# Top-k attention and MLP on one core: when MLP chunks arrive, a scan in place of a merge, and reciprocals on GpSimd

## The chip, the core and the metric

The kernel runs on one core of one Trainium2 chip. The time is the device time of one execution in microseconds (us), the median of several runs. The core has five engines with a queue each: TensorE (PE in the profile; PEld is its loading of weights), VectorE (DVE), ScalarE (ACT), GpSimd (POOL) and SyncE (SP), which here only issues DMA transfers. Each engine works through its own instructions in order; they wait for each other through semaphores.

## What is computed

Attention in which each query keeps only its 32 largest scores, followed by a two-layer MLP. All data is float32.

```python
# q, k, v: (8 batches, 8 heads, 576 positions, 64)
scores = scale * np.matmul(q, k.transpose(0, 1, 3, 2))
kth = np.partition(scores, -32, axis=-1)[..., -32:-31]
scores = np.where(scores >= kth, scores, -1e9)
attn = np.exp(scores - np.max(scores, axis=-1, keepdims=True))
attn = attn / (np.sum(attn, axis=-1, keepdims=True) + 1e-09)
x = (attn @ v) brought to (4608 tokens, 512)
h = x @ w_in                                   # (4608, 2048)
g = np.where(h >= 1, h, np.where(h <= -1, 0.0, (h + 1) ** 2 / 4))
return g @ w_out                               # (4608, 512)
```

## The kernel before

**Tiles and steps.** The 576 positions of a batch are four tiles of 128 and a tail of 64. A step (`steps`, line 471) is 128 queries of two heads. A full tile has four steps (one for each pair of heads); the tails of two batches share one MLP tile, and each tail has two steps, because its 64 queries of two pairs of heads fill 128 partitions. That makes 144 steps. `rounds` (line 462) is the order of the tiles over the pairs of batches.

**One step.** `scores` (line 257): TensorE computes 128x576 scores for each of the two heads, and ScalarE copies them out, scaled, into `s`. `first_top` (line 282) forms `more`, the larger of each pair of scores (score c and score c + 288), finds its 8 largest by VectorE's MAX8, and lets ScalarE take the exponential into `e`. `weights` (line 297) then goes on to the 32 largest of `more`: three rounds of MATCH_REPLACE8, which removes the eight found, and MAX8, which finds the next eight, each for two heads on 128x288. Since only the larger of each pair has been looked at, the smaller ones follow: line 317 forms them, line 320 takes their 8 largest (`seconds`), and lines 321 to 324 merge the two sorted lists. The 32nd largest of the union is the largest of these nine numbers: the 32nd of the first list, and min(first list from its 31st downward in rank, seconds upward) for eight pairs; a 9-element MAX8 for each head finds it (`kth`). The mask (line 330) multiplies `e` by "score at least kth" and sums into `z`.

**The sum's reciprocal.** Lines 335 and 336 add 1e-9 to `z` and take the reciprocal `rz` on VectorE, both on 128x2. After that a step goes one of two ways. While the weights of the MLP are still being converted, and in the last two steps, `by_tensor` is set: ScalarE makes a diagonal matrix of `rz`, and TensorE scales and transposes `e` in one matmul (`transpose_w`). In the other 130 steps GpSimd scales `e` by `rz` (line 343), and `move_w` (line 369) has ScalarE split it in 16-bit halves, writes them to DRAM and reads them back through the transposing DMA into `wT`. `values` (line 381) is the product with v, two steps later, and its result is copied to `xT`, the MLP's input.

**The MLP in chunks.** A chunk (`chunks`, line 462) is one or two tiles of 128 tokens. When its last step has passed `values`, its work is put into `pending`: for each of 16 pieces of the hidden layer, `hidden` (4 blocks of `w_in`, ScalarE and GpSimd for the activation) and, four pieces later, `final` (with `w_out`). A tile is worth 128 units, so there are 36 x 128 = 4608 units in all. A float32 matmul shows as two matmul instructions in the trace.

**The order on the engines** is written out by hand. The loop over steps (line 612) divides each step in 7 slots, and `advance` (line 516) puts in pieces of pending MLP work at the end of each slot. How much is set by `share`:

```python
share = (total - spent) / (n + 2 - m)          # line 619
```

that is, what is left of the MLP, spread over the steps that are left. If `pending` runs out, nothing is put in until the next chunk is complete. `K_TIME` (line 513) is the planner's estimate of the time of a step; it bounds what `advance` puts in, and does not itself wait for anything. In the first steps the weights `w_in` and `w_out`, which arrive as 64-bit numbers, are converted by ScalarE, VectorE and GpSimd along with the attention. At the end a flag says whether the second smallest list was ever too short (`excess`, line 345); a second, plain run follows only then.

Of the kernel before, what the change touches and what calls it, by code (L numbers as in the profile page):

```python
# [10 lines left out]
F32 = mybir.dt.float32  # L11
# [3 lines left out]
AF = mybir.ActivationFunctionType  # L15
ALU = mybir.AluOpType
PSUM = bass.MemoryType.PSUM

TOP_K = 32
LOWEST = -3.0e38  # L20
LARGEST = 3.4028234e38
# [3 lines left out]
def kernel(  # L25
# [10 lines left out]
    nc = tc.nc  # L36
    B, H, S, D = q.shape
    NTOK, DM = out.shape
    DFF = moe_w_in.shape[1]
    P = 128  # L40
# [4 lines left out]
    NT = S // P  # L45
# [6 lines left out]
    NK = DM // P  # L52
    NF = DFF // P
# [5 lines left out]
    const = ctx.enter_context(tc.tile_pool(name="const", bufs=1))  # L59
# [4 lines left out]
    minus = const.tile([P, 1], F32, name="minus")  # L64
# [13 lines left out]
    for i in range(2):  # L78
        v_tails.append([const.tile([P, H, D], F32, name=f"v_tail{i}{x}") for x in range(2)])
        for x in v_tails[i]:  # L80
            nc.gpsimd.memset(x, 0.0)

# [3 lines left out]
    excess = const.tile([P, 2 * n_steps + n_pieces], F32, name="excess")  # L88
# [68 lines left out]
    def run(ctx, paired):  # L157
        xtp = ctx.enter_context(tc.tile_pool(name="xtp", bufs=3))
        stage = ctx.enter_context(tc.tile_pool(name="stage", bufs=2))
        att = ctx.enter_context(tc.tile_pool(name="att", bufs=2))  # L160
# [96 lines left out]
        def scores(st):  # L257
            t, hp, kT, qT = st["t"], st["hp"], st["keys"]["kT"], st["qT"]
            st["s"] = s = att.tile([P, 2, S], F32, name="s", bufs=3)
            for hf in range(2):  # L260
# [9 lines left out]
                                             start=True, stop=True)  # L270
                nc.scalar.activation(s[:, :, c0:c1], sp[:, :, 0:SH], AF.Copy, scale=SCALE)  # L271

        def pairs(st):
            s = st["s"]
            st["more"] = more = att.tile([P, 2, SH], F32, name="more")
            nc.vector.tensor_tensor(out=more, in0=s[:, :, 0:SH], in1=s[:, :, SH:S], op=ALU.max)  # L279


        def first_top(st):
            s = st["s"]
            if paired:
                pairs(st)
            st["tops"] = tops = att.tile([P, 2, TOP_K + 8], F32, name="tops", bufs=3)
            st["e"] = e = att.tile([P, 2, S], F32, name="e", bufs=3)
            nmax = att.tile([P, 2], F32, name="nmax")
            for i in range(2):
                nc.vector.max(out=tops[:, i, 0:8], in_=(st["more"] if paired else s)[:, i, :])  # L290
            nc.scalar.activation(nmax, tops[:, :, 0], AF.Copy, scale=-1.0)
            for i in range(2):
                nc.scalar.activation(e[:, i, :], s[:, i, :], AF.Exp, bias=nmax[:, i:i + 1])  # L293
                yield


        def weights(st, after):
            s, m, tops, e = st["s"], st["m"], st["tops"], st["e"]
            kth = att.tile([P, 2, 8], F32, name="kth", bufs=3)
            if paired:  # L300
                src = rest = less = st["more"]
            else:
                src, rest = s, att.tile([P, 2, S], F32, name="rest", bufs=1)
            for r in range(8, TOP_K, 8):
                for i in range(2):
                    nc.vector.match_replace(out=rest[:, i, :], in_to_replace=tops[:, i, r - 8:r],  # L306
                                            in_values=src[:, i, :], imm_value=LOWEST)
                src = rest
                if r == 8:
                    yield  # L310
                if r + 8 == TOP_K:
                    yield
                    yield from first_top(after) if after is not None else (None, None)
                for i in range(2):
                    nc.vector.max(out=tops[:, i, r:r + 8], in_=src[:, i, :])  # L315
            if paired:
                nc.vector.tensor_tensor(out=less, in0=s[:, :, 0:SH], in1=s[:, :, SH:S], op=ALU.min)  # L317
                seconds = att.tile([P, 2, 8], F32, name="seconds")
                for i in range(2):
                    nc.vector.max(out=seconds[:, i, :], in_=less[:, i, :])  # L320
                nc.vector.tensor_tensor(out=tops[:, :, TOP_K:TOP_K + 8], in0=tops[:, :, TOP_K - 2:TOP_K - 10:-1],
                                        in1=seconds, op=ALU.min)
                for i in range(2):
                    nc.vector.max(out=kth[:, i, :], in_=tops[:, i, TOP_K - 1:TOP_K + 8])  # L324
                last = kth[:, :, 0]
            else:
                last = tops[:, :, TOP_K - 1]
            z = att.tile([P, 2], F32, name="z")
            for i in range(2):
                nc.vector.scalar_tensor_tensor(out=e[:, i, :], in0=s[:, i, :], scalar=last[:, i:i + 1],  # L330
                                               in1=e[:, i, :], op0=ALU.is_ge, op1=ALU.mult,
                                               accum_out=z[:, i:i + 1])
            yield
            rz = att.tile([P, 2], F32, name="rz")
            nc.vector.tensor_scalar(z, z, 1e-9, None, ALU.add)  # L335
            nc.vector.reciprocal(rz, z)  # L336
            if st["by_tensor"]:
                st["rz"] = diag = (late or words).tile([P, 2, P], F32, name="diag", bufs=1)
                for i in range(2):
                    nc.scalar.activation(diag[:, i, :], ident, AF.Copy, scale=rz[:, i:i + 1])  # L340
            else:
                for i in range(2):
                    nc.gpsimd.tensor_scalar(e[:, i, :], e[:, i, :], rz[:, i:i + 1], 1.0, ALU.mult, ALU.mult)  # L343
            if paired:
                nc.gpsimd.tensor_tensor(out=excess[:, 2 * m:2 * m + 2], in0=seconds[:, :, 7], in1=kth[:, :, 0],
                                        op=ALU.subtract)
            yield

# [113 lines left out]
        rounds, chunks = [], []  # L462
        for b in range(0, B, 2):
            a, c, tl = [(b, t) for t in range(NT)], [(b + 1, t) for t in range(NT)], (b, NT)
            if b + 2 < B:
                rounds += a + [tl] + c + [(b + 1, NT)]
                chunks += [a[0:2], a[2:4], c[0:2], c[2:4], [tl]] if b else [[x] for x in a + c + [tl]]
            else:
                rounds += a + [tl, (b + 1, NT)] + c
                chunks += [a[0:2], a[2:4], [tl]] + [[x] for x in c]  # L470
        steps = []
        for b, t in rounds:
            tile_of = (b, t) if t < NT else (b - b % 2, t)
# [4 lines left out]
        n = len(steps)  # L478

        ready = {max(m for m in range(n) if steps[m][3] == ch): ch for ch in range(len(chunks))}  # L480
# [4 lines left out]
        pending = deque()  # L485
        total, spent = sum(len(tiles) for tiles in chunks) * (NK * NF + NF * DM // P), 0
# [23 lines left out]
                inspected += 1  # L510


        K_TIME, PIECE_TIME, UNIT_TIME, SLOTS, EARLY_STEPS, EARLY_SHARE = 10.2, 0.55, 0.218, 7, 4, 32
        pe_time, dve_time, done, scored, ready_at, usable = 9.0, 12.0, {}, {}, {}, {0: 0.0}

        def advance(amount, until):
# [77 lines left out]
        for _ in first_top(state[0]):  # L594
            pass
        next(first)
        begin_at(1)
        next_keys, valued = 1, 0
# [13 lines left out]
        for m in range(n + 2):  # L612
# [3 lines left out]
            elif not early and late is None:  # L616
                conversion.close()
                late = ctx.enter_context(tc.tile_pool(name="late", bufs=1))
            share = (total - spent) / (n + 2 - m)
            top_k, parts = None, [0] * SLOTS  # L620
            if m < n:
                top_k = weights(state[m], state[m + 1] if m + 1 < n else None)
                parts = [1] * SLOTS if early else [1, 1, 0, 1, 1, 1, 1]
                start = max(dve_time, scored[m])
                now_converting = range(SLOTS) if m < EARLY_STEPS else range(0, SLOTS, 2)
                dve_time = start + K_TIME + PIECE_TIME * min(len(now_converting), n_pieces - converted)
                done[m] = dve_time
                state[m]["by_tensor"] = early or m >= n - 2
# [60 lines left out]
    with ExitStack() as inner:  # L689
        run(inner, True)  # L690
    again = nc.values_load(flag[0:1, 0:1], min_val=0, max_val=1)
    with tc.If(again > 0):
        with ExitStack() as inner:
            run(inner, False)
# [27 lines left out]
```

## Time and profile before

| | |
|---|---|
| time, median of 3 runs | 1683.67 us (1682.41 to 1685.46) |
| span of the profiled execution | 1683.5 us |
| TensorE busy | 1549.2 us, 92% |
| VectorE busy | 1550.5 us, 92% |
| ScalarE busy | 1188.2 us, 71% |
| GpSimd busy | 974.8 us, 58% |
| the last mask of a step (VectorE) ends | 1607 us |

Busy time is the time in which an engine had at least one instruction under way, not counting register, branch, semaphore and DMA-issuing instructions. The ends of matmuls are modelled, so a busy TensorE isn't TensorE at its peak. In the page's 40 slices of the span each digit is the busy share in tenths, and PEclk is the clock granted to TensorE in the same way. A row of groups gives line, engine, operation, output and inputs, shape and count, then the busy time of the group in us and the mean of one instruction in ns, then the engine's idle time just before it and what ended most of it. A line of waits names who waited for whom, the total in us, how often, and the longest.

### The profile page before, as it was taken

How to read it: one execution, taken by the hardware profiler on the slowest of the kernel's cores; microseconds unless marked ns; L12 is line 12 of the kernel's file. 1: busy time of each engine (PE TensorE's matmuls, PEld its weight loads, DVE VectorE, ACT ScalarE, POOL GpSimd, SP SyncE). 2: the span in 40 equal slices, each digit the busy share in tenths (PEclk: the TensorE clock that was granted, in tenths of full speed). 3: DMA queues.
4: the chain of work that ended last, by engine and by line, in shares of the span. 5: the costliest groups of instructions: out<-in, count | busy, mean ns of one | idle time of the engine just before them, and what ended most of it. 6: DMA issues, size and time to landing. Idle time of an engine off the chain costs nothing.

```text
span 1683.5 us, 30910 instructions
## 1 busy us (share of the span) xinstructions
PE 1549.2 (92%) x9645; PEld 1050.8 (62%) x9645; DVE 1550.5 (92%) x4875; ACT 1188.2 (71%) x2552; POOL 974.8 (58%) x1720
## 2 busy tenths in 40 slices
PE   5586999999998899979999999979999999999998
PEld 4464666666665666646566766646566666666675
DVE  6999999999999999999999999999999999999922
ACT  5677677777777767777677877767667877767743
POOL 4675677666665554536465755526465765657750
PEclk6698999999998999979999999979999999999999
DMA  9333345455555546554555555554555544544400
GB/s 246 114 98 91 86 132 160 129 151 141 140 154 156 144 135 174 142 157 135 146 159 143 150 142 151 158 158 124 155 150 151 143 131 130 132 133 117 114 27 16
DMA packets 439055, 227.83 MB, mean 135 GB/s; under 512 B 393056, under 2 KB 401248, under 8 KB 438880
## 3 DMA queue, kind: packets, MB, share of 16 engines
q1 hardware_dynamic: 438880, 225.75, 49.4%
q8 instruction: 78, 1.28, 0.3%
q14 instruction: 97, 0.79, 0.2%
HBM read 62.91 MB, written 86.11 MB: 89 GB/s over the span
## 4 chain that ended last, share of the span: by engine, by line
DVE 51%; PE 33%; ACT 7%; issue 3%; POOL 3%; DMA 2%; SPq 1%; DVEq 0%; POOLq 0%; ACTq 0%
PE ph L419 13%; DVE more L306 12%; PE py L444 12%; DVE tops L315 10%; DVE e L330 8%; DVE more L317 4%; DVE seconds L320 4%; DVE tops L290 4%; DVE more L279 4%; PE po L389 3%; PE sp L269 3%; ACT halves L372 2%; ACT e L293 1%; DVE z L335 1%; DVE kth L324 1%
## 5 line engine op out<-in xcount | busy, mean ns | idle before, releaser
L419 PEld LDWEIGHTS ph<-xT,w_in 128*128 128x128 f32 x3328 | 505.1, 195 | 199.0 <-issue 88.5
L419 PE MATMUL ph<-xT,w_in 128*128 128x128 f32 (+1 forms) x3328 | 594.1, 326 | 32.8 <-ACT g L431 18.6
L444 PE MATMUL py<-w_out,g 128*128 128x512 f32 x1152 | 564.3, 605 | 2.0 <-POOL w_out L136 1.8
L423 ACT ACTIVATE r<-ph,half 128x128 f32<-128x128 f32 (+1 forms) x416 | 169.7, 408 | 292.9 <-PE ph L419 237.6
L306 DVE MATCH_REPLACE8 more<-tops,more 128x288 f32<-128x288 f32 x864 | 375.6, 442 | 0.0
L436 POOL TENSOR_SCALAR r<-r 128x128 f32<-128x128 f32 (+1 forms) x392 | 164.9, 421 | 343.4 <-ACT r L423 342.1
L315 DVE MAX8 tops<-more 128x8 f32<-128x288 f32 x864 | 348.9, 445 | 0.0
L343 POOL TENSOR_SCALAR e<-e,rz 128x576 f32<-128x576 f32 x260 | 211.9, 825 | 205.2 <-DVE rz L336 205.2
L372 ACT COPY halves<-e 128x1152 uint16<-128x1152 uint16 x260 | 286.9, 1156 | 14.7 <-POOL e L343 14.0
L444 PEld LDWEIGHTS py<-w_out,g 128*128 128x128 f32 x1152 | 197.4, 191 | 145.9 <-issue 117.8
L438 POOL TENSOR_TENSOR g<-r,g 128x128 f32<-128x128 f32 (+1 forms) x400 | 261.6, 654 | 31.4
L330 DVE SCALAR_TENSOR_TENSOR e<-s,kth,e 128x576 f32<-128x576 f32 x288 | 242.0, 877 | 0.5
L437 POOL TENSOR_TENSOR r<-r 128x128 f32<-128x128 f32 (+1 forms) x392 | 219.0, 559 | 32.7
L293 ACT ACTIVATE e<-s,nmax 128x576 f32<-128x576 f32 x288 | 218.4, 771 | 4.8
L269 PE MATMUL sp<-kT,qT 64*128 64x288 f32 x1024 | 169.0, 447 | 9.9 <-ACT kT L229 9.1
L271 ACT ACTIVATE s<-sp 128x576 f32<-128x576 f32 x288 | 170.0, 642 | 6.6 <-PE sp L269 6.4
L389 PE MATMUL po<-wT,v_in 128*64 128x128 f32 x2048 | 148.5, 287 | 22.1 <-DMA wT<-rows 13.9
L389 PEld LDWEIGHTS po<-wT,v_in 128*64 128x64 f32 x2048 | 115.5, 141 | 80.7 <-issue 18.3
L431 ACT ACTIVATE g<-ph,minus 128x128 f32<-128x128 f32 (+1 forms) x400 | 162.4, 406 | 0.0
L269 PEld LDWEIGHTS sp<-kT,qT 64*128 64x128 f32 x1024 | 91.8, 193 | 84.6 <-issue 40.6
L320 DVE MAX8 seconds<-more 128x8 f32<-128x288 f32 x288 | 118.3, 452 | 13.9
L317 DVE TENSOR_TENSOR more<-s 128x576 f32<-128x576 f32 x144 | 122.4, 850 | 4.9
(88 smaller groups left out, 1349.6 us busy)
## 6 DMA issues: line engine op xcount, KB each, us to landing
rows<-halves SPq DMA_DIRECT2D x130, 576.0 KB, 2.8
raw<-in_moe_w_out_dram SPq DMA_DIRECT2D x52, 256.0 KB, 3.0
raw<-in_moe_w_in_dram SPq DMA_DIRECT2D x48, 256.0 KB, 3.1
k_in<-in_k_dram SPq DMA_DIRECT2D x64, 128.0 KB, 2.9
q_in<-in_q_dram SPq DMA_DIRECT2D x32, 256.0 KB, 3.1
v_in<-in_v_dram SPq DMA_DIRECT2D x8, 1024.0 KB, 6.0
out_dram<-y SPq DMA_DIRECT2D x32, 256.0 KB, 2.6
kT<-in_moe_w_in_dram SPq DMA_DIRECT2D x16, 256.0 KB, 4.5
```

The lines of the kernel that those rows point to most:

```text
L269: nc.tensor.matmul(o[:, a0 - c0:a1 - c0], qT[d, g, :], kT[d, g, k0:k0 + a1 - a0], start=True, stop=True)
L293: nc.scalar.activation(e[:, i, :], s[:, i, :], AF.Exp, bias=nmax[:, i:i + 1])
L306: nc.vector.match_replace(out=rest[:, i, :], in_to_replace=tops[:, i, r - 8:r], in_values=src[:, i, :], imm_value=LOWEST)
L315: nc.vector.max(out=tops[:, i, r:r + 8], in_=src[:, i, :])
L330: nc.vector.scalar_tensor_tensor(out=e[:, i, :], in0=s[:, i, :], scalar=last[:, i:i + 1], in1=e[:, i, :], op0=ALU.is_ge, op1=ALU.mult, acc ...
L343: nc.gpsimd.tensor_scalar(e[:, i, :], e[:, i, :], rz[:, i:i + 1], 1.0, ALU.mult, ALU.mult)
L372: nc.scalar.copy(halves[:, :, i * S:(i + 1) * S], st["e"][:, i, :].bitcast(U16).rearrange("p (k t) -> p t k", t=2))
L389: nc.tensor.matmul(po[j * D:(j + 1) * D], v_in[:, h, c, :] if c < NT else v_tl[0][:, h, :], wT[:, block(j, c)], start=(c == 0), stop=(c == ...
L419: nc.tensor.matmul(ph, w_in[:, kk, f * P:(f + 1) * P], xT[:, kk, c0:c1], start=(kk == 0), stop=(kk == NK - 1))
L437: nc.gpsimd.tensor_tensor(out=r, in0=r, in1=r, op=ALU.mult)
L438: nc.gpsimd.tensor_tensor(out=g, in0=r, in1=g, op=ALU.add)
L444: nc.tensor.matmul(pys[i], gs[f][:, i * P:(i + 1) * P], w_out[:, f, :], start=(f == 0), stop=(f == NF - 1))
```

## The change

It has three parts, all meant to take work off VectorE or to keep TensorE supplied.

1. *Arrival of chunks.* Within a pair of batches both tails now come between the two batches, so that their shared tile is complete in the middle and not at the end. The chunks of the first pair and the last, and of the second batch of the last but one, are single tiles. And the share of a step is now also bounded by what is pending up to the next chunk's arrival. `K_TIME` goes from 10.2 to 10.4.
2. *Merge by one scan.* The list of the largest of both heads and the list of seconds are laid out so that one scan, state = min(max(state, a), b) over 26 elements, gives both heads' 32nd largest; a bound between the halves (-3.0e38 or the largest float) resets it. It replaces the minimum on 128x16 and two MAX8 on 128x9.
3. *Reciprocals on GpSimd.* In the steps that scale on GpSimd, the addition of 1e-9 and the reciprocal move there: z to the power of -1, and one Newton step, rz * (2 - z * rz), to refine it; five instructions on 128x2.

```diff
+    SPLIT = TOP_K // 2
+    LAST = SPLIT + 8
+    second_lists = [const.tile([P, LAST + 1], F32, name=f"seconds{i}") for i in range(2)]
+    for x in second_lists:
+        nc.gpsimd.memset(x, LOWEST)
+        for i in range(2):
+            nc.gpsimd.memset(x[:, i * SPLIT:i * SPLIT + 1], LARGEST)
...
+        def eight(tops, i, r):
+            c = (r // SPLIT * 2 + i) * SPLIT + r % SPLIT
+            return tops[:, c:c + 8]
...
-                seconds = att.tile([P, 2, 8], F32, name="seconds")
+                seconds = second_lists[m % 2]
                 for i in range(2):
-                    nc.vector.max(out=seconds[:, i, :], in_=less[:, i, :])
-                nc.vector.tensor_tensor(out=tops[:, :, TOP_K:TOP_K + 8], in0=tops[:, :, TOP_K - 2:TOP_K - 10:-1],
-                                        in1=seconds, op=ALU.min)
-                for i in range(2):
-                    nc.vector.max(out=kth[:, i, :], in_=tops[:, i, TOP_K - 1:TOP_K + 8])
-                last = kth[:, :, 0]
+                    nc.vector.max(out=seconds[:, (1 - i) * SPLIT + 1:(1 - i) * SPLIT + 9], in_=less[:, i, :])
+
+                nc.vector.tensor_tensor_scan(out=kth, data0=tops[:, 2 * TOP_K - 1 - LAST:2 * TOP_K], data1=seconds[:, LAST::-1],
+                                             initial=LOWEST, op0=ALU.max, op1=ALU.min)
+                last = [kth[:, 8:9], kth[:, LAST:LAST + 1]]
...
-            nc.vector.tensor_scalar(z, z, 1e-9, None, ALU.add)
-            nc.vector.reciprocal(rz, z)
             if st["by_tensor"]:
+                nc.vector.tensor_scalar(z, z, 1e-9, None, ALU.add)
+                nc.vector.reciprocal(rz, z)
                 st["rz"] = diag = (late or words).tile([P, 2, P], F32, name="diag", bufs=1)
...
             else:
+                nc.gpsimd.tensor_scalar(z, z, 1e-9, None, ALU.add)
+                nc.gpsimd.tensor_tensor(out=rz, in0=z, in1=minus.to_broadcast([P, 2]), op=ALU.pow)
+                nc.gpsimd.tensor_tensor(out=z, in0=z, in1=rz, op=ALU.mult)
+                nc.gpsimd.tensor_scalar(z, z, -1.0, 2.0, ALU.mult, ALU.add)
+                nc.gpsimd.tensor_tensor(out=rz, in0=rz, in1=z, op=ALU.mult)
                 for i in range(2):
                     nc.gpsimd.tensor_scalar(e[:, i, :], e[:, i, :], rz[:, i:i + 1], 1.0, ALU.mult, ALU.mult)
...
-            if b + 2 < B:
-                rounds += a + [tl] + c + [(b + 1, NT)]
-                chunks += [a[0:2], a[2:4], c[0:2], c[2:4], [tl]] if b else [[x] for x in a + c + [tl]]
+            rounds += a + [tl, (b + 1, NT)] + c
+            if 0 < b and b + 2 < B:
+                chunks += [a[0:2], a[2:4], [tl]] + ([c[0:2], c[2:4]] if b + 4 < B else [[x] for x in c])
             else:
-                rounds += a + [tl, (b + 1, NT)] + c
-                chunks += [a[0:2], a[2:4], [tl]] + [[x] for x in c]
+                chunks += [[x] for x in a + [tl] + c]
...
-        K_TIME, PIECE_TIME, UNIT_TIME, SLOTS, EARLY_STEPS, EARLY_SHARE = 10.2, 0.55, 0.218, 7, 4, 32
+        K_TIME, PIECE_TIME, UNIT_TIME, SLOTS, EARLY_STEPS, EARLY_SHARE = 10.4, 0.55, 0.218, 7, 4, 32
...
-            share = (total - spent) / (n + 2 - m)
+            share, left = (total - spent) / (n + 2 - m), sum(x[0] for x in pending)
+            for r in sorted(ready):
+                if r + 3 > m and r >= valued:
+                    share = min(share, left / (r + 3 - m))
+                    left += len(chunks[ready[r]]) * (NK * NF + NF * DM // P)
```

More of the change, by code (lines that the diff above doesn't have):

```diff
@@ L285, in first_top @@
                 pairs(st)
-            st["tops"] = tops = att.tile([P, 2, TOP_K + 8], F32, name="tops", bufs=3)
+            st["tops"] = tops = att.tile([P, 2 * TOP_K], F32, name="tops", bufs=3)
             st["e"] = e = att.tile([P, 2, S], F32, name="e", bufs=3)
@@ L289, in first_top @@
             for i in range(2):
-                nc.vector.max(out=tops[:, i, 0:8], in_=(st["more"] if paired else s)[:, i, :])
-            nc.scalar.activation(nmax, tops[:, :, 0], AF.Copy, scale=-1.0)
+                nc.vector.max(out=eight(tops, i, 0), in_=(st["more"] if paired else s)[:, i, :])
+            nc.scalar.activation(nmax, tops[:, 0:2 * SPLIT:SPLIT], AF.Copy, scale=-1.0)
             for i in range(2):
@@ L298, in weights @@
             s, m, tops, e = st["s"], st["m"], st["tops"], st["e"]
-            kth = att.tile([P, 2, 8], F32, name="kth", bufs=3)
+            kth = att.tile([P, LAST + 1], F32, name="kth", bufs=3)
             if paired:
@@ L305, in weights @@
                 for i in range(2):
-                    nc.vector.match_replace(out=rest[:, i, :], in_to_replace=tops[:, i, r - 8:r],
+                    nc.vector.match_replace(out=rest[:, i, :], in_to_replace=eight(tops, i, r - 8),
                                             in_values=src[:, i, :], imm_value=LOWEST)
@@ L314, in weights @@
                 for i in range(2):
-                    nc.vector.max(out=tops[:, i, r:r + 8], in_=src[:, i, :])
+                    nc.vector.max(out=eight(tops, i, r), in_=src[:, i, :])
             if paired:
                 nc.vector.tensor_tensor(out=less, in0=s[:, :, 0:SH], in1=s[:, :, SH:S], op=ALU.min)
-                seconds = att.tile([P, 2, 8], F32, name="seconds")
+                seconds = second_lists[m % 2]
                 for i in range(2):
-                    nc.vector.max(out=seconds[:, i, :], in_=less[:, i, :])
-                nc.vector.tensor_tensor(out=tops[:, :, TOP_K:TOP_K + 8], in0=tops[:, :, TOP_K - 2:TOP_K - 10:-1],
-                                        in1=seconds, op=ALU.min)
-                for i in range(2):
-                    nc.vector.max(out=kth[:, i, :], in_=tops[:, i, TOP_K - 1:TOP_K + 8])
-                last = kth[:, :, 0]
+                    nc.vector.max(out=seconds[:, (1 - i) * SPLIT + 1:(1 - i) * SPLIT + 9], in_=less[:, i, :])
+                nc.vector.tensor_tensor_scan(out=kth, data0=tops[:, 2 * TOP_K - 1 - LAST:2 * TOP_K], data1=seconds[:, LAST::-1],
+                                             initial=LOWEST, op0=ALU.max, op1=ALU.min)
+                last = [kth[:, 8:9], kth[:, LAST:LAST + 1]]
             else:
-                last = tops[:, :, TOP_K - 1]
+                last = [eight(tops, i, TOP_K - 8)[:, 7:8] for i in range(2)]
             z = att.tile([P, 2], F32, name="z")
             for i in range(2):
-                nc.vector.scalar_tensor_tensor(out=e[:, i, :], in0=s[:, i, :], scalar=last[:, i:i + 1],
+                nc.vector.scalar_tensor_tensor(out=e[:, i, :], in0=s[:, i, :], scalar=last[i],
                                                in1=e[:, i, :], op0=ALU.is_ge, op1=ALU.mult,
@@ L344, in weights @@
             if paired:
-                nc.gpsimd.tensor_tensor(out=excess[:, 2 * m:2 * m + 2], in0=seconds[:, :, 7], in1=kth[:, :, 0],
+                nc.gpsimd.tensor_tensor(out=excess[:, 2 * m:2 * m + 2], in0=seconds[:, 8:9 + SPLIT:SPLIT], in1=kth[:, LAST:7:-SPLIT],
                                         op=ALU.subtract)
```

## The prediction

> **What bounds the kernel now.** I read the page's busy shares first, then its 40 slices, then the kernel cut into stages by hand, then one step of VectorE in the timeline, and last the waits.
>
> ```profile
> PE 1549.2 (92%) x9645; PEld 1050.8 (62%) x9645; DVE 1550.5 (92%) x4875; ACT 1188.2 (71%) x2552; POOL 974.8 (58%) x1720
> PE   5586999999998899979999999979999999999998
> DVE  6999999999999999999999999999999999999922
> PEclk6698999999998999979999999979999999999999
> ```
>
> TensorE and VectorE are level at 92%, but not in the same places. The stages say where (columns: stretch, length, then busy time and instructions of each engine, clock, DMA):
>
> ```profile
> 0.00:190.00 190.00, 130.12 (x844) 98.18 (x844) 173.72 (x516) 127.81 (x314) 113.32 (x179) 0.80 0.46 129
> 190.00:520.00 330.00, 314.04 (x2214) 217.56 (x2211) 312.01 (x985) 246.79 (x569) 231.15 (x457) 0.99 0.53 142
> 520.00:920.00 400.00, 370.71 (x2125) 240.47 (x2125) 388.07 (x1239) 286.51 (x565) 206.78 (x333) 0.94 0.55 149
> 920.00:1240.00 320.00, 304.42 (x1767) 201.16 (x1762) 310.43 (x983) 233.43 (x464) 174.16 (x287) 0.96 0.55 147
> 1240.00:1480.00 240.00, 239.21 (x1481) 159.08 (x1480) 233.14 (x737) 177.67 (x361) 145.10 (x239) 1.00 0.53 142
> 1480.00:1607.00 127.00, 121.55 (x816) 84.90 (x816) 122.17 (x385) 89.24 (x205) 83.78 (x174) 0.97 0.42 116
> 1607.00:1683.50 76.50, 69.16 (x417) 49.45 (x411) 10.99 (x40) 26.70 (x81) 20.55 (x55) 0.97 0.04 12
> ```
>
> Three parts. A start of 190 us: the 12 steps that also convert weights, VectorE full. A middle of 1417 us, 132 steps at 10.7 us each: VectorE is busy 97% of every 40 us there (about 38.8, the rest being small gaps between dependent instructions), so it sets the pace, except in 190 to 520, where it is at 95% and waits 8.8 us for scores. TensorE in the middle: 1349.9 of 1417 us, 95.3%. It dips where no finished chunk is left to feed the MLP, at a lower clock (0.94 and 0.96 above), and is full at 239.2 of 240 us in 1240 to 1480. A tail of 76.5 us after the last selection, TensorE alone.
>
> One VectorE step, undisturbed:
>
> ```profile
> 820.53 0.17 DVE L321 TENSOR_TENSOR tops<-tops,seconds 128x16 f32<-128x16 f32 x1
> 820.74 0.24 DVE L324 MAX8 kth<-tops 128x8 f32<-128x9 f32 x2
> 820.95 0.82 DVE L330 SCALAR_TENSOR_TENSOR e<-s,kth,e 128x576 f32<-128x576 f32 x1
> ...
> 822.43 0.08 DVE L330 DVE_READ_ACCUMULATOR e<-s,kth,e 128x1 f32 x1
> 822.54 0.17 DVE L335 TENSOR_SCALAR z<-z 128x2 f32<-128x2 f32 x1
> 822.75 0.17 DVE L336 RECIPROCAL rz<-z 128x2 f32<-128x2 f32 x1
> 822.83 0.07 DVE L306 MATCH_VALUE_LOAD more<-tops,more 128x8 f32 x1
> ```
>
> The start times are what to read: 0.42 us from the small merge to the mask, 0.40 us from the accumulator to the next step's first instruction, of which the two 128x2 operations are nearly all.
>
> ```profile
> PEld po L389 <- DMA wT<-rows: 17.6, 7, 4.4
> POOL e L343 <- DVE rz L336: 205.2, 45, 8.8
> L343 POOL TENSOR_SCALAR e<-e,rz 128x576 f32<-128x576 f32 x260 | 211.9, 825 | 205.2 <-DVE rz L336 205.2
> L345 POOL TENSOR_TENSOR excess<-seconds,kth 128x2 f32<-128x2 f32 x144 | 35.9, 249 | 0.0
> ```
>
> GpSimd waits for VectorE's reciprocal in 45 of the 130 late steps; TensorE waits for the weights that come of it only 7 times. The last row is the nearest thing to the new small GpSimd operations.
>
> [...]an operation on 128x2 costs 166 to 227 ns on VectorE (reciprocal and the addition before it). [...]the two-input mask (median 819 ns) reaches 1280 ns, while the one-input selections stay at 440 to 450 ns. [...]I use TensorE's share only to compare stages of this kernel.
>
> **The change, part by part.**
>
> *Scan for the merge.* Out go a minimum (0.21 us of step) and two 9-element maxima (0.21 us); in comes one scan of 26 elements. Its price isn't in the trace. Lower end: any tiny operation, 0.17 us. Upper end: the two maxima and the minimum it replaces, 0.42. I take 0.25[...]. Saved: 0.17 us in each of 144 steps; 12 in the start, 2.0 us; 132 in the middle, 22 us.
>
> *Reciprocal to GpSimd.* In 130 late steps VectorE loses two operations. From 0.40 us, some 0.07 stays, as between the two masks: 0.33 us, plus 0.06 because the addition averages 227 ns where its median is 169 (it runs into GpSimd's work). 130 x 0.39 = 51 us. GpSimd gets five 128x2 operations: at the 249 ns of the excess row 1.25 us a step, 162 us in all, and its total goes from 975 to about 1137, under 1640. The power is in no trace here: between 0.2 us, as its neighbours, and several us[...]; I take at most 0.5. In GpSimd's queue the scaling of e, the excess and then the MLP's r and g stand behind the five; who waits is ScalarE's copy, the DMA transpose and TensorE's values, two steps later. The path gets 1.25 - 0.35 = 0.9 us longer. That hides in the distance of two steps wherever TensorE is behind (7 waits now); the new operations come while VectorE is in its one-input selections, so I charge no contention.
>
> *Even arrival.* Both tails now run before the second batch, and the share is cut so that chunks last until the next. In the old order a pair of tiles comes after 8, 16, 26 and 34 steps and the tail at 36; at 32 units a step the largest lag before an arrival is 26 x 32 - 512 = 320 units; in the new order it is 256 (8, 16, 20, 28, 36). The starved stretches should fill, and less be left at the end. In the tail TensorE now does 76 of the 1152 second matmuls (line 444 alone, by stretches), 2.4 tiles of 32. With single tiles in the last pair I expect the last tile and some 0.6 more: 0.8 tile moves into the middle, 22 us at 28 us a tile (the tail's hidden and output matmuls repeat every 1.75 us, 16 times a tile). The price is more chunks of one tile: 24 instead of 16. By the rows with shapes kept apart, a single tile takes 128 x 0.136 (278.0 us by 2048) = 17.4 us of first matmuls, half a double 64 x 0.247 (316.1 by 1280) = 15.8: 8 x 1.6 = 13 us more. The planner's step time of 10.4 instead of 10.2 costs nothing by itself: it only lets slightly more MLP in per step, and the share binds first.
>
> **The sum.** VectorE in the middle: 1365.8 busy - 73 = 1293, and over 0.97 for its gaps 1333 us. TensorE in the middle: 1349.9 + 22 + 13 - about 15 (slow clock after starving: 6% of 400 and 4% of 320 is 37 us, part of it idle) = 1370 us. So the load changes places: TensorE becomes the longer of two nearly equal engines. At the fullest seen, 99.7%, it would need 1374; two engines that feed each other two steps ahead won't hold that, and the single-tile stretch shows 95.2%. I take 98%: 1398. With the start 190 - 2 = 188 and the tail 76.5 - 22 = 54: **1640 us**. About 30 us of VectorE's gain vanish behind TensorE, and the rest is had only because the chunks come evenly.
>
> **The rivals.**
> - *VectorE's saving in full.* TensorE's single tiles cost nothing (in the tail a single tile runs at the pace of a double) and the middle takes 1350 / 0.997 = 1354: 188 + 1354 + 54 = 1596 us. For it: 1240 to 1480 ran full with 198 second matmuls of the MLP in 22.5 steps (counted by line 444), 8.8 a step where 8 suffice. Against: the stretch of single tiles, 11.0 us a step, waits for ScalarE and GpSimd.
> - *Single tiles and a busier GpSimd hold TensorE at 96%.* 1370 / 0.96 = 1427: 188 + 1427 + 54 = 1669 us. For it: GpSimd is at 70% in 190 to 520, and 1.25 us more a step makes it 81% with single tiles over a third of the run; "ACT r <- POOL g" already costs 20.5 us in 200 to 520. Against: that idle time is partly VectorE's pace, which falls.
> - *Slower: the power is long.* At 4 us, GpSimd gets about 5 us a step, 650 us, and with 49 more for single tiles (8 x 16 x 0.38 us) 975 + 699 = 1674[...]: 1726 us. For it: the power is the one operation with no row. Against: only two elements in each partition.
>
> **How the numbers follow.** Forecast 0.53, full saving 0.17, held at 96% 0.20, slower 0.10. The predicted time is the forecast's. The range runs from 1602, just short of the full saving, to 1674, just past the third case; the case with a long power is left out, and half of the fastest. Faster 0.87 (the first two and 0.17 of the third), same 0.03 (the third at 95.3% as now ends at 1680), slower 0.10.
>
> **What would show it.** Right: VectorE with some 1475 us busy; the scan at 0.2 to 0.3 us; the power under 0.5 us; TensorE without slices of 7 after the start; VectorE waiting for scores (more on s) well over 11 us; a tail of about 54 us. Wrong: a power of over 1 us, or many waits of values on the DMA transpose, makes it slower; VectorE still at 97% and TensorE with idle time makes it faster than I say.

## The result, and the profile after

The changed kernel takes 1824.7 us, median of four runs (1822.9 to 1829.7), where the kernel before takes 1683.0 us beside it: 1.0844 times as long, with a 95% interval of 1.082 to 1.0869. The prediction was 1640 us, in a range of 1602 to 1674, so it was wrong in sign and far outside.

From the page of the changed kernel: its busy shares, the slices of TensorE and VectorE, and the shares of the chain that ended last.

```profile
PE 1587.3 (87%) x10157; PEld 1078.6 (59%) x10157; DVE 1509.4 (83%) x4327; ACT 1209.3 (66%) x2680; POOL 1263.7 (69%) x2568
PE   5687998898888899898888899988888998899898
DVE  7999899898898879788887879988867786888852
ACT 32%; POOL 26%; PE 24%; DVE 8%; issue 7%; DMA 1%; POOLq 0%; SPq 0%; ACTq 0%; DVEq 0%
```

VectorE was relieved: its busy time is 41 us less. But no engine is full any more. TensorE and VectorE are mostly at 8 where they were at 9. The granted clock isn't the reason: it was 0.957 in this profile and 0.952 in the one before. The chain that ended last, in which VectorE had 51% before, now runs mostly through ScalarE and GpSimd, and neither of these is over 70% busy. That is the picture of engines waiting for each other in turn, and the groups say for what (busy time, mean of one in ns, idle time ahead of it, releaser):

```profile
L392 ACT COPY halves<-e 128x1152 uint16<-128x1152 uint16 x260 | 287.5, 1152 | 206.5 <-POOL e L363 205.9
L294 DVE TENSOR_TENSOR more<-s 128x576 f32<-128x576 f32 x144 | 110.3, 766 | 211.1 <-ACT s L281 211.0
L363 POOL TENSOR_SCALAR e<-e,rz 128x576 f32<-128x576 f32 x260 | 201.7, 786 | 13.4
```

The first two rows had 14.7 and 10.7 us of idle time before. ScalarE now waits 206 us for GpSimd's scaled e, and VectorE 211 us for ScalarE's scores. The third row had 205.2 us of waiting for VectorE's reciprocal; now GpSimd waits for nothing from VectorE in these steps that the profile shows. The small operations, from the groups with shapes kept apart:

```profile
L357 POOL TENSOR_SCALAR z<-z 128x2 f32<-128x2 f32 x130 | 43.7, 336 | 11.0
L358 POOL TENSOR_TENSOR rz<-z,minus 128x2 f32<-128x2 f32 x130 | 99.9, 768 | 10.9
L359 POOL TENSOR_TENSOR z<-z,rz 128x2 f32<-128x2 f32 x130 | 30.0, 231 | 10.2
L360 POOL TENSOR_SCALAR z<-z 128x2 f32<-128x2 f32 x130 | 48.8, 375 | 11.4
L361 POOL TENSOR_TENSOR rz<-rz,z 128x2 f32<-128x2 f32 x130 | 40.5, 311 | 10.8
```

The five sum to 262.9 us, 2.02 us a step, where the prediction had 1.25. One turn of the loop, from the timeline (start, duration, engine and instruction; in brackets the engine's idle time before it, and what ended it):

```profile
605.96 0.50 ACT L443 ACTIVATE r<-ph,half 128x256 f32<-128x256 f32 x1
...
606.55 0.43 POOL L456 TENSOR_SCALAR r<-r 128x256 f32<-128x256 f32 x1 [0.98 <-ACT r L443]
...
607.76 0.73 POOL L458 TENSOR_TENSOR g<-r,g 128x256 f32<-128x256 f32 x1
...
608.33 0.76 DVE L332 TENSOR_TENSOR more<-s 128x576 f32<-128x576 f32 x1
...
608.57 0.61 POOL L357 TENSOR_SCALAR z<-z 128x2 f32<-128x2 f32 x1
...
612.01 1.48 POOL L363 TENSOR_SCALAR e<-e,rz 128x576 f32<-128x576 f32 x2
...
612.80 2.21 ACT L392 COPY halves<-e 128x1152 uint16<-128x1152 uint16 x2 [3.73 <-POOL e L363]
...
615.14 1.44 ACT L308 ACTIVATE e<-s,nmax 128x576 f32<-128x576 f32 x2
616.49 1.17 ACT L281 ACTIVATE s<-sp 128x576 f32<-128x576 f32 x2
...
617.69 0.76 DVE L294 TENSOR_TENSOR more<-s 128x576 f32<-128x576 f32 x1 [1.82 <-ACT s L281]
617.70 0.49 ACT L443 ACTIVATE r<-ph,half 128x256 f32<-128x256 f32 x1
...
620.29 0.61 POOL L357 TENSOR_SCALAR z<-z 128x2 f32<-128x2 f32 x1
```

Follow it downward. GpSimd takes z only after the MLP's r and g that stand ahead of it, and those come when ScalarE gives r. From z to the scaled e it is 4.9 us. ScalarE stands 3.73 us at its copy, with nothing passing it; behind the copy are the exponentials, the scores, and the next r. VectorE waits 1.82 us for those scores, and GpSimd gets its next r at 618. So the turn closes: it takes 11.7 us from z to z, set not by the work of one engine but by a circle through two in-order queues. VectorE is not part of the circle: its mask for the z that GpSimd takes up at 620.29 had ended at 611.86.

### The profile page after: what moved, and what is told of

Same layout as the page of the kernel before. It is cut to its first block, busy times and chain, and to the rows that moved or that the text cites. A ratio compares the mean times of both kernels' runs of the same rounds, so it can differ in the third digit from the quotient of the medians.

```text
span 1823.1 us, 32498 instructions
## 1 busy us (share of the span) xinstructions
PE 1587.3 (87%) x10157; PEld 1078.6 (59%) x10157; DVE 1509.4 (83%) x4327; ACT 1209.3 (66%) x2680; POOL 1263.7 (69%) x2568
## 4 chain that ended last, share of the span: by engine, by line
ACT 32%; POOL 26%; PE 24%; DVE 8%; issue 7%; DMA 1%; POOLq 0%; SPq 0%; ACTq 0%; DVEq 0%
ACT halves L392 11%; PE ph L439 10%; PE py L464 8%; ACT e L308 7%; ACT s L281 5%; POOL e L363 5%; POOL g L458 4%; POOL rz L358 4%; POOL r L457 4%; ACT r L443 3%; PE sp L279 2%; ACT sign L163 2%; POOL z L360 2%; POOL r L456 2%; PE po L409 2%
## 5 line engine op out<-in xcount | busy, mean ns | idle before, releaser
L439 PEld LDWEIGHTS ph<-xT,w_in 128*128 128x128 f32 x3840 | 544.5, 198 | 290.8 <-ACT g L451 114.0
L439 PE MATMUL ph<-xT,w_in 128*128 128x128 f32 (+1 forms) x3840 | 626.1, 310 | 100.8 <-ACT g L451 77.4
L464 PE MATMUL py<-w_out,g 128*128 128x512 f32 x1152 | 582.3, 612 | 9.2 <-POOL g L458 8.5
L392 ACT COPY halves<-e 128x1152 uint16<-128x1152 uint16 x260 | 287.5, 1152 | 206.5 <-POOL e L363 205.9
L456 POOL TENSOR_SCALAR r<-r 128x128 f32<-128x128 f32 (+1 forms) x456 | 195.6, 429 | 326.2 <-ACT r L443 325.0
L443 ACT ACTIVATE r<-ph,half 128x128 f32<-128x128 f32 (+1 forms) x480 | 187.2, 390 | 294.6 <-PE ph L439 195.8
L294 DVE TENSOR_TENSOR more<-s 128x576 f32<-128x576 f32 x144 | 110.3, 766 | 211.1 <-ACT s L281 211.0
L458 POOL TENSOR_TENSOR g<-r,g 128x128 f32<-128x128 f32 (+1 forms) x464 | 248.4, 535 | 36.5
L344 DVE SCALAR_TENSOR_TENSOR e<-s,kth,e 128x576 f32<-128x576 f32 x288 | 256.7, 927 | 6.0
L363 POOL TENSOR_SCALAR e<-e,rz 128x576 f32<-128x576 f32 x260 | 201.7, 786 | 13.4
L451 ACT ACTIVATE g<-ph,minus 128x128 f32<-128x128 f32 (+1 forms) x464 | 179.6, 387 | 0.0
```

Source lines behind the costliest of these rows:

```text
L392: nc.scalar.copy(halves[:, :, i * S:(i + 1) * S], st["e"][:, i, :].bitcast(U16).rearrange("p (k t) -> p t k", t=2))
L439: nc.tensor.matmul(ph, w_in[:, kk, f * P:(f + 1) * P], xT[:, kk, c0:c1], start=(kk == 0), stop=(kk == NK - 1))
L458: nc.gpsimd.tensor_tensor(out=g, in0=r, in1=g, op=ALU.add)
L464: nc.tensor.matmul(pys[i], gs[f][:, i * P:(i + 1) * P], w_out[:, f, :], start=(f == 0), stop=(f == NF - 1))
```

## The experiments

Theory Q, formed on this profile: the five operations hold e back, ScalarE's copy waits for it at the head of its queue, and what is behind it comes late. There are two rivals. Theory S: the new single-tile chunks are too much for ScalarE and GpSimd. Theory L: GpSimd's load is too much, wherever the copy stands. All times are medians; the kernel before ran beside each at 1682.8 to 1684.7 us.

**no_recip** undoes the third part of the change alone.

```diff
-                nc.gpsimd.tensor_scalar(z, z, 1e-9, None, ALU.add)
...
+                nc.vector.tensor_scalar(z, z, 1e-9, None, ALU.add)
+                nc.vector.reciprocal(rz, z)
```

> The changed kernel with the reciprocals back on VectorE; even arrival and scan stay. Theory Q (the five GpSimd operations hold e back, ScalarE's copy of the halves waits for it at the head of its queue, and the scores behind it reach VectorE late): the copy's wait for GpSimd falls from 206 us to under 30, VectorE's wait for scores from 211 to under 30, and the time to 1630 to 1665 us. Theory S (the single tiles of the new chunks are what ScalarE and GpSimd can't follow): the time stays above 1750 us.

1665.7 us, 0.991 of before (0.9886 to 0.9934). Its waits:

```profile
DVE more L294 <- ACT s L281: 22.5, 18, 3.9
ACT halves L389 <- POOL e L360: 16.2, 23, 2.1
```

Both fell as Q said, and the time is 0.7 us above what it expected. On top of the first two parts the third costs 159 us, and the first two together gain 17. So S falls: without the reciprocals on GpSimd the same single tiles do no such harm.

**recip_only** makes the third part the only change to the kernel before (the same lines, the other way).

> The kernel before with the reciprocals on GpSimd as the only change. Theory Q: the loss comes with it, 1780 to 1840 us, with the copy's wait for GpSimd rising from 14 to over 150 us. Theory S: under 1700 us, since the chunks are the old ones.

1791.4 us, 1.0642 (1.0624 to 1.066). The loss comes with the reciprocals: 109 us on the old chunks. The copy's wait rose to 134.6 us only, a little under what Q expected. The third part is thus 50 us dearer beside the other two than alone. No run takes this apart; after_pairs, below, shows that the number of single tiles is a small share of it.

**no_newton** takes three of the five operations away, so the reciprocal is left as the power gives it.

```diff
-                nc.gpsimd.tensor_tensor(out=z, in0=z, in1=rz, op=ALU.mult)
-                nc.gpsimd.tensor_scalar(z, z, -1.0, 2.0, ALU.mult, ALU.add)
-                nc.gpsimd.tensor_tensor(out=rz, in0=rz, in1=z, op=ALU.mult)
```

> The changed kernel without the three operations of the Newton step: the reciprocal is left at what the power gives. GpSimd loses about 0.9 us a step by the rows (0.23 + 0.38 + 0.31). Theory Q: e comes 0.9 us earlier in 130 steps, and as the delay stands in a loop of GpSimd and ScalarE nearly all of it comes off: 1700 to 1740 us. Theory S: no more than 10 us off.

1723.9 us, 101 us less than the changed kernel, as Q expected. The three rows hold 119 us, and 85% of that came off the end, though GpSimd is busy only 69% of the time. The copy's wait is 112.2 us, VectorE's 99.7.

**late_move** puts ScalarE's copy two slots later in the step, behind the next scores.

```diff
-                if slot == 2 and 1 <= m <= n and not state[m - 1]["by_tensor"]:
-                    move_w(state[m - 1])
-                    ready_at[m - 1] = done[m - 1] + 14.0
...
+                if slot == 4 and 1 <= m <= n and state[m - 1] is not None and not state[m - 1]["by_tensor"]:
+                    move_w(state[m - 1])
+                    ready_at[m - 1] = done[m - 1] + 14.0
```

> The changed kernel with ScalarE's copy of the halves put two slots later, behind the scores of the step after next; GpSimd's five operations stay. Theory Q: what hurts is that the copy waits at the head of ScalarE's queue; with it later most of the loss goes, under 1700 us, and VectorE's wait for scores falls from 211 to under 60 us. Theory L (GpSimd's load itself[...] is too much wherever the copy stands): above 1770 us. Values may wait for the DMA transpose more, by up to 3 us a step, under both.

1886.4 us, slower still: Q in this form fell, and the time is what L expected. The copy waits only 0.8 us for e now, yet VectorE waits, and more than before:

```profile
DVE more L294 <- ACT s L281: 293.1, 100, 7.6
ACT r L443 <- POOL g L458: 150.9, 80, 5.9
PE po L409 <- DMA wT<-rows: 68.6, 45, 4.1
```

ScalarE now stops at another place. It writes r into one of two buffers, and GpSimd, occupied with the block of z and e, hasn't freed one; that wait was 69.7 us in the changed kernel. And values now wait for the later transpose. So there are two ways in which GpSimd can hold ScalarE: e comes late (theory E), or the MLP's pieces are delayed behind the block (theory O, occupation, which is L with a place for its wait). The next four runs tell them apart.

**r_three** and **late_r_three** give the changed kernel and late_move a third r buffer.

```diff
-                r = pool.tile([P, CW], F32, name="r", bufs=2)[:, 0:c1 - c0]
+                r = pool.tile([P, CW], F32, name="r", bufs=3)[:, 0:c1 - c0]
```

> The changed kernel (1825 us) with three r buffers in place of two. Theory O: ScalarE can be one piece of the MLP further ahead of GpSimd, its wait on GpSimd's g falls from 70 to under 30 us, and the time falls by at least 40 us. Theory E: the copy at the head of ScalarE's queue still waits, less than 15 us off.

> late_move (1886 us) with three r buffers. There the copy no longer waits for e, but ScalarE waits 151 us for GpSimd's g. Theory O: that wait falls under 80 us, and the time under 1800 us. Theory E has no reason why late_move was slow and none for a change here: within 20 us of 1886.

r_three: 1797.1 us, 28 us off, between the two expectations. ScalarE's wait for g fell from 69.7 to 16.9 us, while the copy's rose from 205.9 to 222.0 us. late_r_three: 1788.9 us, 98 us off, with the wait for g at 32 us: the buffer was what late_move ran against, and with it the later copy ends 36 us below the changed kernel. With both places eased the kernel is still 123 us slower than no_recip. Values wait there for the transpose (61.8 us in the largest group), and scores still come late (191.7 us); what these 123 us are made of, no run shows.

**dummy_after** is no_recip with the same five operations, on two tiles that nobody reads, behind the scaling of e in GpSimd's queue. **dummy_before** has them in front of it. Nothing else differs between the two. The diff is that of dummy_after against no_recip; the lines left out make the two tiles and do the Newton step on them.

```diff
                 for i in range(2):
                     nc.gpsimd.tensor_scalar(e[:, i, :], e[:, i, :], rz[:, i:i + 1], 1.0, ALU.mult, ALU.mult)
+            if not st["by_tensor"]:
...
+                nc.gpsimd.tensor_scalar(z2, rz, 1e-9, None, ALU.add)
+                nc.gpsimd.tensor_tensor(out=r2, in0=z2, in1=minus.to_broadcast([P, 2]), op=ALU.pow)
...
```

> The reciprocals on VectorE, as in no_recip (1666 us), and behind GpSimd's scaling of e the same five small operations on two tiles that nobody reads: they add no part of the computation. Same load of GpSimd as in the changed kernel, but e isn't held back by them. Theory O (occupation: GpSimd's in-order queue makes the MLP's r and g behind the five wait, and ScalarE, with two r buffers, then waits for GpSimd in front of the scores): at least 1750 us. Theory E (it is the lateness of e, at which ScalarE's copy waits): within 25 us of no_recip, under 1690 us.

> dummy_after (1730 us) with the five idle operations in front of the scaling of e in GpSimd's queue and not behind it; all else, VectorE's reciprocal too, is the same. They add no part of the computation. Theory E for the remainder (lateness of e, on top of occupation): 1805 to 1850 us, near the changed kernel, with ScalarE's copy waiting over 150 us for GpSimd. If occupation is all that the five do: within 15 us of 1730.

dummy_after: 1730.3 us, between the two expectations; dummy_before: 1816.8 us (1811.1 to 1824.5), as theory E had it. First dummy_after's waits, then dummy_before's:

```profile
ACT r L447 <- POOL g L462: 84.1, 51, 6.4
DVE more L294 <- ACT s L281: 81.4, 42, 7.1
ACT halves L396 <- POOL e L360: 19.3, 30, 2.1
```

```profile
ACT halves L395 <- POOL e L366: 189.2, 94, 5.4
DVE more L294 <- ACT s L281: 136.7, 58, 6.9
```

This splits the loss. From 1665.7 to 1730.3 us, 65 us: occupation of GpSimd (with what VectorE's instructions lose beside GpSimd's: its busy time is 1536.2 us in dummy_after and 1530.1 in no_recip), seen as ScalarE's wait for g, which was 26.4 us in no_recip. From 1730.3 to 1816.8 us, 86 us: the same work in a worse order, seen as the copy's wait for e. The five operations don't run slower in that order: they hold 245.4 us in dummy_before and 260.7 in dummy_after. VectorE does lose something: its busy time is 1559.4 us in dummy_before and 1536.2 in dummy_after. So a part of the 86 us can be this loss; the copy's wait, up from 19.3 to 189.2 us, is the far larger change. The last 8 us, to 1824.7, are about the spread of the runs. In the changed kernel VectorE is relieved of its two operations, and that relief bought nothing. L as a whole falls too: the load alone, in the better order, costs 65 us of the 159.

**after_pairs** is the changed kernel with two-tile chunks in the second batch of the third pair and the first batch of the last: 16 single tiles instead of 24.

```diff
-            if 0 < b and b + 2 < B:
-                chunks += [a[0:2], a[2:4], [tl]] + ([c[0:2], c[2:4]] if b + 4 < B else [[x] for x in c])
+            if b:
+                chunks += [a[0:2], a[2:4], [tl]] + ([c[0:2], c[2:4]] if b + 2 < B else [[x] for x in c])
```

> The changed kernel with 16 single tiles in place of 24, as in no_add_pairs; GpSimd has 49 us less of the MLP's work. If the single tiles only add their own cost: 28 us off, 1790 to 1802 us. If they are what makes the five operations so dear: under 1760 us.

1815.1 us, 10 us off, less than either expectation: the loss stands with the old number of single tiles.

**arrival_only** and **scan_only** make one of the other two parts the only change to the kernel before.

> The kernel before with the even arrival alone (order of tiles, chunks, share, planner's step time). The prediction's account: TensorE's starved stretches fill and the tail loses about 22 us, but VectorE still sets the pace in the middle at 10.7 us a step, so only the tail's part shows: 1655 to 1668 us. Rival (the single tiles cost what the tail gains): 1675 to 1690 us.

> The kernel before with the scan alone. By starts in the timeline the scan takes the place of 0.42 us a step with some 0.3: if VectorE sets the pace, 0.12 to 0.17 us by 144 steps, 17 to 24 us off in the middle, but TensorE stays starved in the same places and the tail takes up what is not done earlier: 1664 to 1678 us. Rival (TensorE's work alone sets the end): 1680 to 1686 us.

arrival_only: 1682.1 us, 0.999 (0.9984 to 0.9997). This is a miss of its first expectation; the rival, that the single tiles cost what the tail gains, gave the right range. Its slices have no starved stretch left, as planned, and the tail is 63 us where it was 76. But the last mask ends at 1616 us and not at 1607: VectorE has the same 1550.5 us of work and waits 19.9 us for scores, where it waited 10.7. scan_only: 1672.4 us, 0.9927 (0.9914 to 0.994), inside the first range; VectorE's busy time fell by 14.0 us, to 1536.5.

**no_add** leaves the addition of 1e-9 out of no_recip in the late steps; it rounds away, since z is at least 1. **no_add_pairs** adds the chunks of after_pairs, **no_add_r_three** the third r buffer to no_add, **no_add_pairs_r_three** both.

```diff
-                nc.vector.tensor_scalar(z, z, 1e-9, None, ALU.add)
                 nc.vector.reciprocal(rz, z)
```

> no_recip without the addition of 1e-9 in the late steps: the sum holds the largest element's exp(0) = 1, and 1 + 1e-9 rounds to 1 in float32, so nothing changes in the numbers. It frees VectorE of one small operation, 0.17 to 0.23 us a step, 22 to 30 us in 130 steps. If VectorE still sets the pace in no_recip: 1640 to 1648 us. If TensorE does, as the prediction had it: 1655 to 1666 us.

> no_add (1657.6 us), with chunks of two tiles also in the second batch of the third pair and the first batch of the last: 16 single tiles as in the kernel before, and not 24, in the new even order. If single tiles cost TensorE 1.6 us each and hold the late stretch up by waits for ScalarE and GpSimd, 10 to 20 us off: 1638 to 1648 us. If what they save in the tail and in evenness is worth as much: 1652 to 1665 us.

> no_add (1657.6 us) with three r buffers. ScalarE waits there 41 us for GpSimd's g, and TensorE 42 us for ScalarE behind it. If that coupling is what holds TensorE at 95 to 97% in the stretch of single tiles: 1640 to 1650 us. If TensorE's own work sets the end: 1653 to 1660 us.

> no_add_pairs (1629.6 us) with three r buffers, which took 14 us off no_add. ScalarE's wait for GpSimd's g is 24 us there and was 41 in no_add, so the buffer should bring less: 1618 to 1627 us; nothing, within 2 us of 1630, if VectorE sets the pace there at its 97%.

no_add: 1657.6 us. VectorE lost 18.6 us of work (1530.1 to 1511.5) and the kernel 8 us: VectorE alone doesn't set the pace there, and the time is in the range given for TensorE. no_add_pairs: 1629.6 us (0.9665, 0.9652 to 0.9678), 28 us off and more than expected. TensorE's busy time fell by only 12 us, but VectorE's wait for scores fell from 38.5 to 10.7 us, and the wait of TensorE's first matmuls for ScalarE's g from 41.7 to 29.0: the eight single tiles cost more through waits than through their own matmuls. It is likely that arrival_only's gain went the same way, but that isn't shown: two-tile chunks with the even order alone were not run, and in after_pairs they bring only 10 us. no_add_r_three: 1643.7 us, 14 us off, as the account by coupling had it. no_add_pairs_r_three: 1620.2 us (0.9621, 0.9603 to 0.9639), also as expected, the fastest of all, and faster than both kernels. Its page:

```profile
PE 1516.4 (94%) x9645; PEld 1032.6 (64%) x9645; DVE 1500.8 (93%) x4457; ACT 1185.1 (73%) x2552; POOL 975.9 (60%) x1726
PE   5586999999999999999999999999999999999998
DVE  7999999999999999999999999999999999999922
```

TensorE and VectorE are both at 9 to the end of the middle, and GpSimd has the load of the kernel before (974.8 us there).

## Why the prediction was wrong

**The step that failed** is in the reciprocal to GpSimd: "That hides in the distance of two steps wherever TensorE is behind". It followed the lateness to the far consumer, TensorE's values, and took the margin there. That margin held: in the changed kernel the matmuls of values wait for the transpose 5.6 and 3.7 us in their two groups. But the near consumer, ScalarE's copy, has no such margin. It was named as one that waits, and what stands behind it in ScalarE's own queue was not: exponentials, scores and the MLP's r. In the profile before, the copy seldom waited:

```profile
ACT halves L372 <- POOL e L343: 14.0, 11, 2.9
```

But a short wait doesn't mean a wide margin. In the same trace, from the end of e's first half to the start of its copy it is 1.86 us at the median of the 130 steps, and in 32 of them it is less than the 0.9 us by which the prediction made the path longer. In the changed kernel the copy waits 95 times. dummy_before against dummy_after puts 86 us on this, the largest part of the 159.

**The load as a total.** "under 1640" was the wrong test for GpSimd. At 1263.7 of 1823 us it isn't the bound by its sum, and still 65 us come from occupation. Two r buffers let ScalarE run only two pieces ahead while GpSimd is at the block of z and e; r_three shows that this place is worth 28 us in the changed kernel.

**Sizes and overlaps.** The five operations took 2.02 us a step, not 1.25. The power is 718 ns at the median (the guess was "at most 0.5"), and up to 1282 beside an instruction of VectorE; the others are 191 to 224 ns at their medians, near the excess row, but average up to 375. "I charge no contention" failed with its premise, that they come in VectorE's one-input selections. GpSimd reaches z late, and 77 of the 130 powers overlap a mask or one of VectorE's TENSOR_TENSOR instructions, which have two inputs; the other 53 took 718 to 721 ns. In the turn shown above, the operation on z at 608.57 starts beside such an instruction, ends just after it, and takes 0.61 us where its median is 0.22. All 179 of the changed kernel's small operations, the excess row's among them and the power left out, that took over 0.4 us end 0.05 to 0.08 us after such an instruction; those that overlap none took at most 0.25.

VectorE pays as well. The two operations that it lost held 50.5 us in no_recip, and the prediction took off 51. But its busy time in the changed kernel is only 20.7 us less than in no_recip, since its scans went from 39.6 to 57.8 us and its masks from 248.4 to 256.7. VectorE ended at 1509.4 us, not at "some 1475".

**The slower rival** was on the list, at 0.10, for another reason: a power of 4 us that would fill GpSimd. With the measured 2.02 us that sum gives no loss; that GpSimd would then be busy in 1674 of 1726 us was the author's estimate, and no run here fills it. The sign came out as in that case, the mechanism did not. Neither of the two signs that the prediction named for a slower kernel was seen: the power stayed under 1 us at the median, and values waited for the transpose 8 times in those two groups.

**What held.** The scan: 210 ns at least and 274 at the median in the changed kernel, in the predicted 0.2 to 0.3. The 0.25 was the author's estimate within the two ends that the trace before gave, 0.17 and 0.42. It has 25 elements; the description of the change and the prediction counted 26. Its saving was over-sized: scan_only shows 14.0 us of VectorE's busy time, 0.10 us a step, not 0.17. The even arrival did fill the starved slices (the granted clock of arrival_only's profile is 0.973, where the one before has 0.952), but the tail fell to 63 to 66 us, in arrival_only and in the changed kernel, and not to 54. The term "8 x 1.6 = 13 us" for single tiles was right for TensorE's own work (12 us from no_add to no_add_pairs), but the time came down by 28 us: the waits that single tiles bring were missing from the sum. That the load would pass from VectorE to TensorE is half right: no_add shows that VectorE wasn't alone the bound, but no_add_pairs shows that much of what held TensorE was the waits at small pieces, not its sum of work.

## What to carry to other kernels

When a small operation moves to an idle engine, look at the first instruction that waits for its result, and at all that is queued behind that instruction on its engine; slack further down didn't help here: the copy's wait rose from 14.0 to 205.9 us while values waited 9.3 us for the transpose. A circle of in-order queues can set the pace with every engine under 90%, as here, where the busiest is at 87%: look for it where the chain that ended last runs through the less busy engines. Put work that only fills an engine behind the instruction that others wait for (dummy_after against dummy_before: 86 us), and count the buffers that let its neighbour run ahead.

## What the runs showed of the hardware

In the changed kernel, a power on GpSimd for 128x2 takes 718 ns at the median where a product takes 194. Small operations of two elements there stretch from about 0.2 to as much as 0.85 us beside a mask or a TENSOR_TENSOR of VectorE, and those over 0.4 us end 0.05 to 0.08 us after it. A scan over 25 elements takes 210 to 215 ns on VectorE in the 14 steps in which nothing on GpSimd overlaps it, and up to 694 in the others. In the kernel before, the mask takes 806 to 820 ns where nothing on GpSimd overlaps it, and up to 1280 beside a TENSOR_TENSOR there. The granted clock in the profile before, in stretches of 40 us, was 0.70 from 720 to 760 us, where TensorE was busy for 28.0 us, 0.83 from 520 to 560 us (32.2 us busy), and 1.00 in every stretch in which it was busy throughout.
